# Softmax weighting with V stationary in four column tiles, one group of four heads at a time, turned back by one DMA transposition

## The chip, the cores and the metric

The kernel runs on one core of a Trainium2 chip. The metric is device time in microseconds (us), as the median of the runs of one kernel. The engines are called as in the profile: PE (TensorE matmul) and PEld (its weight loads), DVE (VectorE), ACT (ScalarE), POOL (GpSimd), SP (SyncE, which here only issues DMAs). SBUF is the working memory, PSUM the memory that PE's results go to; a bank is a piece of PSUM that holds one 128x512 fp32 tile here.

## The reference

`x` has 2048 rows of D = 640, in bf16. It is normalised by a layer norm and goes through two branches, whose product is added to `x`:

```python
xn = layernorm(x)
# branch A: 32 heads of Dh = 20, four segments of L = 512 rows
for s in range(4):
    p = softmax(qs @ ks.T * scale + causal_mask)          # inside the segment
    a_dot = p @ vs
    a_mem = (phi(qs) @ M) / (phi(qs) @ z + 1e-6)          # memory of earlier segments
    o = g * a_mem + (1 - g) * a_dot                       # g = sigmoid(beta), one per head
    M += phi(ks).T @ vs;  z += phi(ks).sum(rows)
s = concat(o) @ wo
# branch B: gated linear unit, F = 1536
g = silu((sigmoid(xn @ w_gate) * (xn @ w_up)) @ w_down)
out = x + s * g
```

## The kernel before

**Segments and slots.** The four segments follow each other. Each has 20 slots: four pairs of head groups (a group is four heads, so there are eight groups) times five score batches, `UNITS`. A slot begins with one batch, `scores`: for four heads at once, in four row tiles of the PE array (24 rows each), it writes scores transposed, keys on the partitions, into `Sps`, a PSUM tile of four banks that exists once. ACT takes the exponential of all four banks in one instruction (L527) into `pt` in SBUF, and POOL masks the diagonal blocks of `pt` in place (L530). The causal lower half is never computed, so a group has ten blocks of 128 keys by 128 queries per head: 512 + 384 + 256 + 128 = 1280 query columns. Batches 0 and 3 of `UNITS` hold 512 columns of one group each; batch 1 holds the 128 and 384 of the first group, batch 4 those of the second, and batch 2 the 256 of both.

**Weighting.** `weigh` (L535 on) multiplies by V. For each block and head one matmul has the 128x128 block of `pt` as the stationary operand and the head's 21 columns of `V` (20 and a column of ones) as the moving one, into `Aps`, one PSUM bank that exists once: 40 matmuls a group. The 21st column gives the softmax denominator. After a group's last block DVE takes the reciprocal (L553), multiplies by 1 - g (L554), and writes the product into `od` (L556), with queries on the partitions. A batch is weighed one slot after its scores, in the middle of that slot; the second part of batch 2 one slot later still (`due`, `held`).

**Around it.** The rest of a segment's work is put between by two means. Tasks with a time (in slots) lie in heaps: `at(time, cost, fn)`, and `later` for steps that follow others. Those that cost PE time (`tasks`: V, K and Q projections, the output projection `o_proj`, the memory's read and update) may run in both halves of a slot, those of no cost (`soft`: DMAs, DVE and ACT steps) only in the second half. The gated unit's matmul groups are `bulk`: `gate` and `up` (five matmuls of 512 columns, 1.09 each in the planner) and `down` (twelve of 320, 1.64). A planner gives each slot a level of PE time: `level` minus what the slot already holds, `fixed`, of which `PASS` is the part for weighting. 45% of a slot's share (`FIRST`) is run straight after the scores, then the weighting that is due, then `phi` steps, then soft tasks and the rest:

```python
pt = scores(n, pair, u)
delay[0] = True
goal += FIRST * share
fill(now + 0.45, (tasks,))
flush()
for w in due:
    weigh(*w)
```

All other PSUM tiles come from `ps_d`, three banks in rotation (`dtile`). A `gate` bank is released by ACT's tanh (L431), an `up` bank by DVE (L442), a `down` bank by ACT (L459) and then DVE (L461). While `delay[0]` is true, projections are copied out by DVE, otherwise by ACT (`evacuate`).

**DMAs.** Nearly all are issued by SP, in program order: loads, the store of K and Q to DRAM and their return in another layout (`stage_out` L310, `relay` L274, `c_in` L353), and three families of DMA transpositions: `xn` into `xnT` (L263, L265), `phi(k)` into `pkt` (L378, 128x512 bf16 each), `od` into `oT` (L475, four a segment). `o_ready` adds the memory's part to `od` and lets `o_turn` issue the latter; `o_proj` reads `oT`.

Of the kernel before, what the change touches and what calls it, by code (L numbers as in the profile page):

```python
# [9 lines left out]
P = 128  # L10
S = 2048
D = 640
H = 32
DH = 20
VW = DH + 1
KR = DH + 4
NSEG = 4
L = 512
F = 1536
DC = D // P  # L20
FC = F // P
NG = 8
# [4 lines left out]
BF = mybir.dt.bfloat16  # L27
F32 = mybir.dt.float32
U16 = mybir.dt.uint16
ACT = mybir.ActivationFunctionType  # L30
ALU = mybir.AluOpType
# [19 lines left out]
NU = len(UNITS)  # L51
NSLOT = NG // 2 * NU
WARM = 40
FIRST = 0.45
PASS = [0.41, 0.41, 0.41, 0.2, 0.61]
R = NSLOT / 24


@with_exitstack
def kernel(  # L60
# [14 lines left out]
    nc = tc.nc  # L75
# [3 lines left out]
    cpool = ctx.enter_context(tc.tile_pool(name="const", bufs=1))  # L79
# [3 lines left out]
    lnp = ctx.enter_context(tc.tile_pool(name="ln", bufs=2))  # L83
    xpool = ctx.enter_context(tc.tile_pool(name="xpool", bufs=2))
    stg = ctx.enter_context(tc.tile_pool(name="stg", bufs=1))
    ptp = ctx.enter_context(tc.tile_pool(name="ptp", bufs=3))
    opool = ctx.enter_context(tc.tile_pool(name="opool", bufs=2))
    gpool = ctx.enter_context(tc.tile_pool(name="gpool", bufs=2))
    fpool = ctx.enter_context(tc.tile_pool(name="fpool", bufs=2))
# [13 lines left out]
    def at(time, cost, fn, *a):  # L103
        count[0] += 1
        heapq.heappush(first if fn is phi else tasks if cost > 0.1 else soft, (time, count[0], cost, fn, a))
# [75 lines left out]
                            base=0, pattern=[[-1, P]], channel_multiplier=1)  # L181
    V = []
    for i in range(8):
        va = cpool.tile([P, H, VW], BF, name=f"va{i}")
        V.append(va)
    QT = [cpool.tile([P, 4, L], BF, name=f"QT{i}") for i in range(3)]
    KT = [cpool.tile([P, 4, L], BF, name=f"KT{i}") for i in range(3)]
    nInd = cpool.tile([P, DC, H], F32, name="nInd")
# [3 lines left out]
    def v_ones(a, b):  # L192
        for i in range(a, b):
            nc.gpsimd.memset(V[i][:, :, DH:VW], 1.0)

    def make_ind():

# [116 lines left out]
    def q_chunk(n, c):  # L314
        s = st[n]
        if c == 0:
            s["q5"] = stg.tile([P, DC, L], BF, name="q5")
            s["aq"] = stg.tile([P, DC, L], BF, name="aq")
        ps = dtile([P, L], F32, "psq")
        for k in range(DC):  # L320
            nc.tensor.matmul(ps[:], lhsT=W["q"][:, k, c * P:(c + 1) * P], rhs=s["xnT"][:, k, :],  # L321
                             start=(k == 0), stop=(k == DC - 1))
        (nc.vector.tensor_copy if n else nc.scalar.copy)(s["q5"][:, c, :], ps[:])
        nc.vector.tensor_scalar(s["aq"][:, c, :].bitcast(U16), s["q5"][:, c, :].bitcast(U16), 0x7FFF, None,
                                op0=ALU.bitwise_and)
        if c in (2, 4) and n:
            later(0.9, stage_out, n, c // 4, Qs, QT, "q5")
# [141 lines left out]

    def o_turn(n, j, parts):  # L470
        if "oT" not in st[n]:
            st[n]["oT"] = fpool.tile([P, 4, DC, P], BF, name="oT", bufs=1)
        dst = st[n]["oT"][:, j, 0:parts, :]
        src = st[n]["od"][:, j, 0:parts * P]
        later(0.7, lambda: nc.sync.dma_start_transpose(dst, src))  # L475
# [58 lines left out]
    def weigh(n, pair, u, dg, pt):  # L534
        s = st[n]  # L535
        g = 2 * pair + dg
        first = (u, dg) in ((0, 0), (2, 1))
        if first:
            s["A"] = ps_a.tile([P, 4, 4, VW], F32, name="Aps")
        A = s["A"]  # L540

        mine = [(kb, c0) for (d, kb, c0, ncol) in UNITS[u] if d == dg]
        blocks = [(kb, c0 + (qb - kb) * P, qb) for (kb, c0) in mine for qb in range(kb + 1, 4)]
        blocks += [(kb, c0, kb) for (kb, c0) in mine]
        for (kb, off, qb) in blocks:
            for r in range(4):
                nc.tensor.matmul(A[:, qb, r, :], lhsT=pt[:, r, off:off + P],  # L547
                                 rhs=V[4 * (n % 2) + kb][:, 4 * g + r, :],
                                 start=first, stop=True, skip_group_check=True)
                first = False  # L550
        if (u, dg) in ((2, 0), (4, 1)):
            rd = opool.tile([P, 4, 4], F32, name="rd", bufs=3)
            nc.vector.reciprocal(rd[:], A[:, :, :, DH])  # L553
            nc.vector.tensor_tensor(rd[:], rd[:], gin["omg"][:, 4 * g:4 * g + 4].unsqueeze(1).to_broadcast([P, 4, 4]),  # L554
                                    op=ALU.mult)
            nc.vector.tensor_tensor(  # L556
                s["od"][:, :, 4 * g * DH:(4 * g + 4) * DH].rearrange("p q (r e) -> p q r e", e=DH),
                A[:, :, :, 0:DH], rd[:].unsqueeze(3).to_broadcast([P, 4, 4, DH]), op=ALU.mult)


    bulk = [(1.09, fn, (0, f)) for f in range(FC) for fn in (gate, up)]
# [77 lines left out]
    for n in range(NSEG):  # L639
        w = NSLOT * n  # L640
        m = n + 1
        if m < NSEG:
            if n:
                for p in range(2):
                    for i in range(2):
                        at(w + (-1.4, -0.7, 0.1, 0.55)[2 * p + i], 0.1, ln_stats, m, p, i, i + 1)
                        at(w + (0.6, 0.9, 1.7, 2.0)[2 * p + i], 0.1, ln_norm, m, p, i)
            for i in range(8):
                at(w + R * (3.5 + (0.6 * i if i < 4 else 2.5 + 0.55 * (i - 4))), 0.68, v_tile, m, i // 2, i % 2)
            for c in range(DC):  # L650
                at(w + R * (8.8 + 1.0 * c if n else 9.4 + 0.9 * c), 1.08, k_chunk, m, c)
                at(w + R * (13.8 + 1.1 * c), 1.08, q_chunk, m, c)
                if m + 1 < NSEG:
                    at(w + R * (12.8 + 0.85 * c), 0.0, phi, m, "k5", c)
                at(w + R * (17.4 + 0.8 * c), 0.0, phi, m, "q5", c)
            at(w + R * 19.2, 0.6, q_bound, m)
            if m + 1 < NSEG:
                for p in range(2):
                    at(w + R * (16.1 + p), 0.0, x_load, m + 1, p)
            if n == 0:  # L660
                for c in range(DC):
                    at(R * (2.6 + 0.8 * c), 0.0, phi, 0, "k5", c)
            for i, cs in enumerate(([0, 1, 2], [3, 4])):
                at(w + (9.05, 11.0)[i], 0.75 - 0.25 * i, m_update, n, cs)
        if n >= 1:
            for j in range(4):
                at(w + R * (1.1 + 0.3 * j), 0.0, o_ready, n - 1, j)
                at(w + R * (4.0 + 0.5 * j if j < 3 else 9.6), 0.0, xr_load, n - 1, j)
            for i in range(8):
                at(w + R * (5.4 + 1.1 * i), 0.68, o_proj, n - 1, i // 2, i % 2)  # L670
                at(w + (R * (3.4 + 0.85 * i) if i < 6 else i + 1.55), 0.25, mem_read, n, i // 2, i % 2)
# [13 lines left out]
        while tasks or soft or first:  # L685
            run_task(min((h for h in (tasks, soft, first) if h), key=lambda h: h[0][:2]))

    due, held = [], []
    for n in range(NSEG):
        st[n]["od"] = opool.tile([P, 4, D], BF, name="od")  # L690
        if n:
            bulk += [(1.09, fn, (n, f)) for f in range(FC) for fn in (gate, up)]
        bulk += [(1.64, down, (n, j, h)) for j in range(4) for h in range(2)]
        keep = 4 if n >= NSEG - 2 else 0

        left = sum(b[0] for b in bulk[:len(bulk) - keep])
        fixed = [PASS[i % NU] + sum(t[2] for t in tasks if i <= t[0] - NSLOT * n < i + 1) for i in range(NSLOT)]
        level = min(fixed)
        while sum(max(level - f, 0.0) for f in fixed) < left:
            level += 0.01  # L700
        given, goal = 0.0, 0.0

        def fill(until, heaps):
            nonlocal given
            while True:
                ready = [h for h in heaps if h and h[0][0] < until]
                if ready:
                    run_task(min(ready, key=lambda h: h[0][:2]))
                if len(bulk) > keep and given + 0.5 * bulk[0][0] <= goal:
                    cost, fn, a = bulk.pop(0)  # L710
                    given += cost
                    fn(*a)
                elif not ready:
                    break

        for slot in range(NSLOT):
            pair, u = divmod(slot, NU)
            now = NSLOT * n + slot
            share = max(level - fixed[slot], 0.0)
            pt = scores(n, pair, u)  # L720
            delay[0] = True
            goal += FIRST * share
            fill(now + 0.45, (tasks,))
# [3 lines that stand above are left out]
            delay[0] = False  # L727
            while first and first[0][0] < now + 1.0:
                run_task(first)
            due, held = held, []  # L730
            due.append((n, pair, u, UNITS[u][0][0], pt))
            if u == 2:
                held.append((n, pair, u, 1, pt))
            goal += (1.0 - FIRST) * share
            fill(now + 1.0, (tasks, soft))
        while len(bulk) > keep:
            cost, fn, a = bulk.pop(0)
            fn(*a)
# [47 lines left out]
```

## Time and profile before

| | |
|---|---|
| Time, median of 3 runs (lowest to highest) | 337.55 us (337.18 to 338.45) |
| Profiled execution: span, first to last instruction | 335.5 us |
| PE, ACT, DVE, POOL busy | 328.2, 226.2, 223.1, 111.4 us |
| Weighting: L547, PE | 1280 matmuls, 44.5 us busy, 173 ns each (pipelined) |
| Exponentials: L527, ACT | 80, 150.1 us, 1877 ns each |
| Granted TensorE clock, mean | 0.999 |

For the profiled execution the page gives the span alone. The runs' median lies 2.05 us above that span, and that much is taken to lie around it. A PE matmul's duration in the profile runs from its start to the end of its pipeline, so neighbours overlap; what a matmul costs PE is the distance from its start to the next one's start. ACT and DVE instructions overlap too, by about 0.1 us. The segments' first score batches start at 32.8, 101.0, 181.6 and 255.9 us; the last slot's work ends near 318 us.

### The profile page before, as it was taken

Reading aid. Unit: us, or ns where it says so; the run is one execution under the profiler, and the core shown is the slowest. Engines: PE = TensorE matmul, PEld = TensorE weight load, DVE = VectorE, ACT = ScalarE, POOL = GpSimd, SP = SyncE. Lnnn points to the kernel's source line nnn. Section 1 sums busy time; section 2 is a strip of 40 time slices with the busy share of each in tenths; the row PEclk is TensorE's granted clock in tenths of the full one; section 3 lists DMA queues with packets and bytes.
Section 4 is the critical chain, followed back from the end, with each engine's and each line's share of the span. In section 5 each row is a group of like instructions: output and inputs, shape, how many; then the busy total and the mean of one; then the engine's idle time right before and its main releaser. Section 6 shows DMA issues by size and latency. Waiting matters only on the chain.

```text
span 335.5 us, 8363 instructions
## 1 busy us (share of the span) xinstructions
PE 328.2 (98%) x3402; PEld 187.0 (56%) x3402; DVE 223.1 (66%) x532; ACT 226.2 (67%) x237; POOL 111.4 (33%) x157
## 2 busy tenths in 40 slices
PE   8999899999999999999999999999999999999995
PEld 7544455555664565654566466654556665544673
DVE  6276356589877677788756977875663686643365
ACT  2653797788786676477686676466887776786730
POOL 6636232323226222332233523342222323223214
PEclk9999999999999999999999999999999999999999
DMA  7955993774821631136720452052220621210032
GB/s 236 355 179 174 292 127 67 235 217 113 201 74 21 119 99 41 49 109 92 223 73 2 57 117 85 25 165 76 72 70 3 90 75 37 77 42 3 2 62 78
DMA packets 54725, 35.53 MB, mean 106 GB/s; under 512 B 28576, under 2 KB 54688, under 8 KB 54688
## 3 DMA queue, kind: packets, MB, share of 16 engines
q1 hardware_dynamic: 52480, 32.23, 38.3%
q10 hardware_dynamic: 2208, 2.79, 2.5%
q8 instruction: 26, 0.43, 0.6%
q14 instruction: 11, 0.09, 0.1%
HBM read 20.19 MB, written 8.39 MB: 85 GB/s over the span
## 4 chain that ended last, share of the span: by engine, by line
PE 85%; DVE 6%; DMA 3%; ACT 2%; issue 1%; SPq 1%; POOL 0%; DVEq 0%; ACTq 0%; POOLq 0%
PE up L438 14%; PE gp L428 14%; PE yp L456 12%; PE Aps L547 9%; PE Sps L522 7%; PE sp L502 7%; PE psk L289 7%; PE psv L360 6%; PE psq L321 5%; DMA Wu<-in_B_w_up_dram 2%; PE wps L571 2%; PE dm L388 1%; PE am L410 1%; DMA Qs<-q 1%; DVE q L374 1%
## 5 line engine op out<-in xcount | busy, mean ns | idle before, releaser
L527 ACT ACTIVATE pt<-Sps 128x2048 bf16<-128x2048 f32 x80 | 150.1, 1877 | 28.2 <-PE Sps L522 26.1
L530 POOL TENSOR_SCALAR_AFFINE_SELECT pt<-pt 128x1024 bf16<-128x1024 bf16 (+1 forms) x80 | 76.8, 960 | 196.4 <-ACT pt L527 196.4
L438 PE MATMUL up<-xnT,Wu 128*128 128x512 bf16 x240 | 59.7, 379 | 0.7 <-DMA Wu<-in_B_w_up_dram 0.7
L428 PE MATMUL gp<-xnT,Wg 128*128 128x512 bf16 x240 | 59.6, 379 | 0.2
L442 DVE SCALAR_TENSOR_TENSOR hT<-tg,up 128x512 bf16<-128x512 bf16 x48 | 32.7, 682 | 36.8 <-PE up L438 30.9
L456 PE MATMUL yp<-Wd,hT 128*128 128x320 bf16 x384 | 57.1, 299 | 0.0
L547 PEld LDWEIGHTS <-pt 128*128 128x128 bf16 x1280 | 43.2, 96 | 14.7 <-DVE od L556 1.3
L431 ACT ACTIVATE tg<-gp 128x512 bf16<-128x512 f32 x48 | 28.6, 596 | 27.4 <-PE gp L428 25.1
L547 PE MATMUL Aps<-va,pt 128*128 128x21 bf16 x1280 | 44.5, 173 | 0.4 <-DVE od L556 0.4
L456 PEld LDWEIGHTS <-hT 128*128 128x128 bf16 x384 | 35.4, 97 | 15.2 <-issue 2.4
L438 PEld LDWEIGHTS <-Wu 128*128 128x128 bf16 x240 | 21.2, 97 | 24.2 <-issue 2.6
L461 DVE SCALAR_TENSOR_TENSOR aa<-t,yp 128x320 bf16<-128x320 bf16 x32 | 15.5, 484 | 27.4 <-ACT t L459 27.3
L428 PEld LDWEIGHTS <-Wg 128*128 128x128 bf16 x240 | 21.0, 97 | 21.8 <-issue 1.7
L522 PE MATMUL Sps<-QT,KT 24*128 24x128 bf16 (+3 forms) x512 | 31.7, 301 | 0.3
L459 ACT ACTIVATE t<-yp 128x320 bf16<-128x320 f32 x32 | 14.0, 438 | 19.6 <-PE yp L456 18.4
L360 PE MATMUL psv<-Wv,xnT 128*128 128x320 bf16 x160 | 26.4, 299 | 0.1
L502 PE MATMUL sp<-Wo,oT 128*128 128x320 bf16 x160 | 25.9, 300 | 0.0
L321 PE MATMUL psq<-xnT,Wq 128*128 128x512 bf16 x100 | 24.3, 380 | 0.0
L289 PE MATMUL psk<-xnT,Wk 128*128 128x512 bf16 x100 | 24.2, 379 | 0.0
L522 PEld LDWEIGHTS <-KT 24*128 24x128 bf16 x512 | 9.2, 92 | 23.4 <-issue 21.7
L504 DVE SCALAR_TENSOR_TENSOR aa<-aa,sp 128x320 bf16<-128x320 bf16 x32 | 15.5, 485 | 7.6 <-PE sp L502 7.5
L502 PEld LDWEIGHTS <-oT 128*128 128x128 bf16 x160 | 14.4, 97 | 8.2 <-issue 2.6
(74 smaller groups left out, 327.5 us busy)
## 6 DMA issues: line engine op xcount, KB each, us to landing
KT<-Ks SPq DMA_DIRECT2D x32, 80.0 KB
QT<-Qs SPq DMA_DIRECT2D x32, 80.0 KB
xr<-in_A_x_dram SPq DMA_DIRECT2D x15, 160.0 KB
out_dram<-xr SPq DMA_DIRECT2D x15, 160.0 KB
xt<-in_A_x_dram SPq DMA_DIRECT2D x6, 320.0 KB
Wg<-in_B_w_gate_dram SPq DMA_DIRECT2D x3, 640.0 KB
Wu<-in_B_w_up_dram SPq DMA_DIRECT2D x3, 640.0 KB
Wd<-in_B_w_down_dram ACTq DMA_DIRECT2D x1, 1920.0 KB
```

Source lines behind the costliest of these rows:

```text
L289: nc.tensor.matmul(ps[:], lhsT=W["k"][:, k, c * P:(c + 1) * P], rhs=s["xnT"][:, k, :], start=(k == 0), stop=(k == DC - 1))
L321: nc.tensor.matmul(ps[:], lhsT=W["q"][:, k, c * P:(c + 1) * P], rhs=s["xnT"][:, k, :], start=(k == 0), stop=(k == DC - 1))
L360: nc.tensor.matmul(ps[:], lhsT=s["xnT"][:, k, j * P:(j + 1) * P], rhs=W["v"][:, k, half * HB:(half + 1) * HB], start=(k == 0), stop=(k == ...
L428: nc.tensor.matmul(gp[:], lhsT=Wg[f // 4][:, k, fo:fo + P], rhs=s["xnT"][:, k, :], start=(k == 0), stop=(k == DC - 1))
L438: nc.tensor.matmul(ps[:], lhsT=Wu[f // 4][:, k, fo:fo + P], rhs=s["xnT"][:, k, :], start=(k == 0), stop=(k == DC - 1))
L442: empty(lambda: nc.vector.scalar_tensor_tensor(out=h[:], in0=tg[:], scalar=1.0, in1=ps[:], op0=ALU.add, op1=ALU.mult))
L456: nc.tensor.matmul(yp[:], lhsT=s["hT"][f][:, j * P:(j + 1) * P], rhs=W["d"][:, f, hs], start=(f == 0), stop=(f == FC - 1))
L502: nc.tensor.matmul(sp[:], lhsT=s["oT"][:, j, c, :], rhs=W["o"][:, c, hs], start=(c == 0), stop=(c == DC - 1))
L522: nc.tensor.matmul(Sps[:, r, c0:c0 + ncol], lhsT=kt[32 * r:32 * r + KR, gi, kb * P:(kb + 1) * P], rhs=qt[32 * r:32 * r + KR, gi, kb * P:L] ...
L527: nc.scalar.activation(pt[:], Sps[:], ACT.Exp, scale=SCALE)
L530: nc.gpsimd.affine_select(out=diag, in_=diag, compare_op=ALU.is_ge, fill=0.0, base=0, pattern=[[0, 4], [0, cnt], [1, P]], channel_multipli ...
L547: nc.tensor.matmul(A[:, qb, r, :], lhsT=pt[:, r, off:off + P], rhs=V[4 * (n % 2) + kb][:, 4 * g + r, :], start=first, stop=True, skip_grou ...
```

## The change

For 30 of the 32 groups the weighting is done per group, with the operands exchanged. `weigh_group` holds V stationary: for each of the four key blocks, four matmuls, one per head, each with 32 columns of V (the head's 21 and the first 11 of the next head, for which V gets one more head of ones) in one of four column tiles of the PE array, and up to 512 columns of `pt` moving. The 16 matmuls of a group write one PSUM bank, `AT`, with the four heads on the partitions and the queries along the row. ACT copies it to `ats` in bf16, one DMA transposition (SP) turns it into `A` in SBUF, with queries on the partitions, and `divide` does the three DVE instructions that `weigh` did, now from `A`.

The place in the order changes as well. A group is weighed straight behind a score batch: the first group of a pair behind batch 3, the second behind batch 0 of the next pair. The transposition is a soft task 0.7 slots after the slot's start, the division one 1.45 slots after. The last pair of the last segment keeps the old way. The planner's `PASS` gives way to `TURN = 0.65` in the slots that weigh. `pt` has four buffers instead of three; `od` has one buffer instead of two, and `oT` shares its place with `aq`. `o_ready` moves from 0.92 to 1.67 slots into the next segment to 1.7 to 2.45.

```diff
+TURN = 0.65
+LAST = (NSEG - 1, NG // 2 - 1)
...
-    ptp = ctx.enter_context(tc.tile_pool(name="ptp", bufs=3))
+    ptp = ctx.enter_context(tc.tile_pool(name="ptp", bufs=4))
...
-        va = cpool.tile([P, H, VW], BF, name=f"va{i}")
-        V.append(va)
+        V.append(cpool.tile([P, H + 1, VW], BF, name=f"va{i}"))
...
             nc.gpsimd.memset(V[i][:, :, DH:VW], 1.0)
+            nc.gpsimd.memset(V[i][:, H, 0:DH], 1.0)
...
-            s["aq"] = stg.tile([P, DC, L], BF, name="aq")
+            s["aq"] = stg.tile([P, DC, L], BF, name="aq", tag="aq")
...
-            st[n]["oT"] = fpool.tile([P, 4, DC, P], BF, name="oT", bufs=1)
+            st[n]["oT"] = stg.tile([P, 4, DC, P], BF, name="oT", tag="aq")
...
         if (u, dg) in ((2, 0), (4, 1)):
-            rd = opool.tile([P, 4, 4], F32, name="rd", bufs=3)
...
+            divide(n, g, A)
+
+    def divide(n, g, A):
+        s = st[n]
+        if "od" not in s:
+            s["od"] = opool.tile([P, 4, D], BF, name="od", bufs=1)
+        rd = opool.tile([P, 4, 4], F32, name="rd", bufs=3)
+        nc.vector.reciprocal(rd[:], A[:, :, :, DH])
+        nc.vector.tensor_tensor(rd[:], rd[:], gin["omg"][:, 4 * g:4 * g + 4].unsqueeze(1).to_broadcast([P, 4, 4]),
+                                op=ALU.mult)
+        nc.vector.tensor_tensor(
+            s["od"][:, :, 4 * g * DH:(4 * g + 4) * DH].rearrange("p q (r e) -> p q r e", e=DH),
+            A[:, :, :, 0:DH], rd[:].unsqueeze(3).to_broadcast([P, 4, 4, DH]), op=ALU.mult)
+
+
+    def weigh_group(now, n, pair, dg, pts):
+        g = 2 * pair + dg
+        AT = ps_a.tile([P, L], F32, name="AT", tag="A")
+        mine = sorted((kb, u, c0, ncol) for u in range(NU) for (d, kb, c0, ncol) in UNITS[u] if d == dg)
+        for i, (kb, u, c0, ncol) in enumerate(mine):
+            v = V[4 * (n % 2) + kb][:].rearrange("p h e -> p (h e)")
+            for r in range(4):
+                h0 = (4 * g + r) * VW
+                nc.tensor.matmul(AT[32 * r:32 * r + 32, kb * P:L], lhsT=v[:, h0:h0 + 32],
+                                 rhs=pts[u][:, r, c0:c0 + ncol],
+                                 start=(i == 0), stop=(i == 3), tile_position=(0, 32 * r))
+        ats = opool.tile([P, L], BF, name="ats", bufs=2)
+        nc.scalar.copy(ats[:], AT[:])
+        A = opool.tile([P, 4, 4, 32], BF, name="Asb", bufs=2)
+        at(now + 0.7, 0.0, lambda: nc.sync.dma_start_transpose(A[:].rearrange("p q r e -> p q (r e)"), ats[:]))
+        at(now + 1.45, 0.0, divide, n, g, A)
...
-                at(w + R * (1.1 + 0.3 * j), 0.0, o_ready, n - 1, j)
+                at(w + 1.7 + 0.25 * j, 0.0, o_ready, n - 1, j)
...
+    def passes(n, i):
+        pair, u = divmod(i, NU)
+        turned = TURN if u == 3 and not old(n, pair) or u == 0 and (n or pair) else 0.0
+        return turned + (PASS[u] if old(n, pair) and u else 0.0)
...
             pt = scores(n, pair, u)
+            if u == 0 and (n or pair):
+                q = n * (NG // 2) + pair - 1
+                weigh_group(now, q // (NG // 2), q % (NG // 2), 1, pts)
+                pts = {}
+            pts[u] = pt
+            if u == 3 and not old(n, pair):
+                weigh_group(now, n, pair, 0, pts)
...
-            due.append((n, pair, u, UNITS[u][0][0], pt))
-            if u == 2:
-                held.append((n, pair, u, 1, pt))
+            if old(n, pair):
+                due.append((n, pair, u, UNITS[u][0][0], pt))
+                if u == 2:
+                    held.append((n, pair, u, 1, pt))
```

## The prediction

> **What bounds the kernel now.** First the page's totals and its chain of waits; after the span, shares of the span by engine:
>
> ```profile
> span 335.5 us, 8363 instructions
> ...
> PE 328.2 (98%) x3402; PEld 187.0 (56%) x3402; DVE 223.1 (66%) x532; ACT 226.2 (67%) x237; POOL 111.4 (33%) x157
> ...
> PE 85%; DVE 6%; DMA 3%; ACT 2%; issue 1%; SPq 1%; POOL 0%; DVEq 0%; ACTq 0%; POOLq 0%
> ```
>
> PE is the bound, so PE time saved counts unless a wait takes its place. An average hides where, so next the windows by segment (columns: window; length, then busy us of PE, PEld, DVE, ACT, POOL; clock; DMA share; GB/s), and two dense stretches:
>
> ```profile
> 32.80:101.00 68.20, 66.71 (x738) 37.31 (x737) 46.87 (x100) 55.59 (x59) 19.27 (x20) 1.00 0.70 167
> 101.00:181.60 80.60, 80.60 (x848) 45.52 (x847) 59.46 (x144) 55.01 (x57) 25.86 (x36) 1.00 0.36 86
> 181.60:255.90 74.30, 74.20 (x800) 41.16 (x799) 54.14 (x131) 51.03 (x48) 24.14 (x32) 1.00 0.30 76
> 255.90:318.00 62.10, 62.02 (x725) 35.19 (x725) 34.53 (x85) 46.21 (x40) 17.55 (x19) 1.00 0.19 44
> ...
> 72.00:98.00 26.00, 25.77 (x289) 15.21 (x285) 22.94 (x48) 21.20 (x26) 8.46 (x8) 1.00 0.58 145
> 132.00:162.00 30.00, 30.00 (x299) 15.47 (x296) 25.56 (x58) 19.60 (x20) 8.86 (x12) 1.00 0.40 95
> ```
>
> In the first segment ACT is at 82%; in the two stretches DVE is at 88 and 85%, and in the first of them the chain in order of time lies on DVE (79.6 to 84.6, 88.7 to 91.4 us). There PE time saved is worth little. Third, PE's timeline of one window (start, us, instruction):
>
> ```profile
> 241.01 0.33 PE L522 MATMUL Sps<-QT,KT 24*128 24x384 bf16 x4
> 241.27 0.60 PE L334 MATMUL cps<-aq,IK 128*32 128x512 bf16 x5
> 241.81 1.25 PE L428 MATMUL gp<-xnT,Wg 128*128 128x512 bf16 x5
> 242.90 0.56 PE L547 MATMUL Aps<-va,pt 128*128 128x21 bf16 x16
> 243.31 0.38 PE L438 MATMUL up<-xnT,Wu 128*128 128x512 bf16 x1
> ```
>
> This has the price of the old weighting (16 in 243.31 - 242.90), of a 512-column matmul (five in 242.90 - 241.81), and a column-tiled product: `cps`, four tiles and then the first again, 32 columns each. Last, a slot's rhythm:
>
> ```profile
> 39.76 0.40 PE L522 MATMUL Sps<-QT,KT 24*128 24x256 bf16 x8
> 40.36 1.87 ACT L527 ACTIVATE pt<-Sps 128x2048 bf16<-128x2048 f32 x1
> 42.30 1.10 POOL L530 TENSOR_SCALAR_AFFINE_SELECT pt<-pt 128x1024 bf16<-128x1024 bf16 x1 [2.69 <-ACT pt L527]
> ```
>
> The next batch can overwrite `Sps` 2.44 us after a batch began (the shortest slots of the trace are 2.44), and `pt` is masked 3.64 us after (43.40 - 39.76).
>
> **Part by part.** *Removed:* 40 matmuls a group at 0.41/16 = 25.6 ns, 1.025 us; 30 groups, 30.8 us.
>
> *Added on PE:* 1280 columns a group if the four heads run side by side. 1.09/5/512 = 0.426 ns a column makes 0.545 us. `cps` took 0.54 for two rounds of 512 (0.436), so 0.10 is the change of tiling. 0.645 us a group, 30 groups 19.4. One after another the tiles would take 2.18 + 0.10; `cps` says not, since its five would have taken 1.09. PE net: **-11.4**.
>
> The Trainium skill ("TensorE: Matmul & The Clock Gate", Measured speedup vs the span model) gives three column tiles of 512 columns a speedup of 2.38, not 3. By that share, as an estimate, four would give 3.17 and a group 0.79 us, so that PE would win 7.1 and not 11.4. The trace disagrees: the five of `cps` in 0.54 are a full four.
>
> *Moved: waits for the mask.* The old weighting of a batch came in the middle of the next slot; now it stands straight behind that slot's scores, where PE has nothing else to do. For the first group of a pair, batch 2 is the late one and is needed after scores (0.33) and two rounds (0.38): PE waits when slot 2 is shorter than 3.64 - 0.71 = 2.93. For the second it is batch 4, after 0.33 and one round: below 3.09. The slots' lengths follow from the kernel's own planner: fixed tasks, weighting and the bulk groups that fall to the slot, plus 0.40 for the scores. For the kernel before that gives 3.67, 3.05, 3.87 for slots 2 to 4 of the first segment, and the trace has 3.68, 3.07, 3.88. For the changed one, short before a weighting are: slot 9 of the first segment (2.23), 14 of the third (2.57), 2, 4, 9 and 14 of the last (2.29, 2.67, 2.17, 2.58). Lifted to 2.44 where shorter, they wait 0.65, 0.52, 0.49, 0.42, 0.65, 0.51: 3.2. Slots under 2.44 wait for `Sps` itself: five, together 1.0, against 0.5 before (2.09 and 2.24). **+3.7**; bounds 1.5 (half the short slots fill up from delays elsewhere) and 5.
>
> *Added on ACT:* 30 copies of 128x512 fp32; the same form, `cb` L337, took 0.58: 17.4 us. In the queue a copy stands behind that slot's exponential, so PE's matmuls are done before ACT gets there; behind it stand the tanh that release `gate` and `down` banks. By segment ACT would hold 59.7 of 64.9, 59.6 of 77.6, 55.6 of 71.3 and 50.3 of 59.8 us. Slack covers it except in the first segment. There slots 2 to 5 hold four exponentials, two copies, five `phi` exponentials (0.63), two tanh (0.6) and four casts (0.43), 14.7 us less 0.1 overlap each, 13.0, in 12.0 us of PE work, and slots 15 to 17 hold 9.5 in 8.5. Part of that can run late: **+1.7**; bounds 0.5 and 4 (half the deficit of an ACT-bound segment).
>
> *Added on SP, DMA and DVE:* the nearest row is the transposition of `pkt`, the same shape: 15 of them held SP 1.19 us at the median, and by the semaphore steps of the trace landed 2.3 to 2.6 us after issue on quiet queues, 3.5 to 4.3 on busy ones. `ats` is ready 3.05 us after the slot's start (2.47, then 0.58), so `A` lands at 5.5 to 7.3. The division is queued on DVE for the second half of the next slot, which DVE reaches at 4.5 to 6. So DVE, in order, waits up to 2 us, and behind it are queued the `hT` and `aa` evacuations that free `ps_d`'s banks, and `phi`'s DVE steps. PE feels that only after two more tiles (2 x 1.09 + 0.33 less 0.68 for L442): some 1.8 us are free, and a DVE that is behind doesn't wait at all. Not covered are three kinds of groups. The first, where SP is held:
>
> ```profile
> 46.36 1.34 SPq L353 DMA_DIRECT2D QT<-Cs  x4
> 47.80 8.76 SPq L378 DMA_TRANSPOSE pkt<-k  x5
> ```
>
> its transposition, due at 46.9, gets behind one of `pkt`, issues at 49 and lands at 52, while DVE is free at 48: 1.2 us on PE. The first group of the second and third segments, which gets behind eight transpositions of `xnT` and `oT` (106.96 to 117.4 before, now 0.8 slots later): 0.4 each. Two groups in the stretch 72 to 98, where DVE is the chain: 0.35 each. **+2.7**; bounds 0 and 12 (a third of the groups at 1.2). What waits on SP behind a transposition (`relay`, `stage_out`, `pkt`) was planned a slot ahead of its use, `o_proj` comes 2 slots after the last `oT`; if that cover were gone, each would cost its 1.2.
>
> *At nothing:* the divisions have the same shapes (0.25 + 0.24 + 0.49), from SBUF; extra memsets lie beside the startup; shared `aq` and `oT` are free half a slot before reuse; `od`'s one buffer is free before the first division, which waits longer for `A`. Bounds -1 and +1.
>
> Sum: -11.4 + 3.7 + 1.7 + 2.7 = -3.3 on the profiled execution, 332.2 for a span of 335.5. With the 2.05 that lie around it: **334.2 us**.
>
> **Rivals.** *All waits are hidden (14%).* Delays lengthen the short slots, so masks are ready, and DVE's waits stay inside the 1.8 us. -11.4 plus 1.5 and 1.5: 329.2. For it: PE shows hardly a stall in the middle segments. Against: the short slots come out of the planner's costs.
>
> *The savings are eaten just so (16%).* ACT in the first segment and DVE in its second half hold the time, so that segment's 3.6 is lost and its waits remain: 337.5.
>
> *The division's wait becomes the bound: slower (27%).* A transposition that lands 4 us after issue, as pkt's did at 153.9, behind one other on SP (1.2), puts `A` at 8.3 us while DVE is there at 5: 3.3 against the 1.8 that the banks allow. It decides once DVE's wait passes 1.8 us. If ten groups pay 1.5 each and the DVE stretches (56 us, at 87%) lose another 2, the sum is -11.4 + 3.7 + 1.7 + 17 = +11, at half of that +2.5: 340 to 348.5, of which 343 is taken. Against: the DMA share is 0.36 and less after the first segment.
>
> *The four tiles don't run side by side (5%).* With 128 rows from four places of `pt` at a share of 3/4, a group costs 0.83 and PE wins 5.9: 339.7; one after another, 2.28 a group, 375 (1%). `cps` speaks against both.
>
> **How the numbers follow.** The forecast has 38%, the rivals 14, 16, 27 and 5. Faster are forecast and first rival, 0.52; the second, 0.16, is no change within 0.5% (1.7 us, about what runs of this kernel can tell: they lie 1.3 apart); slower 0.32. The range 329 to 343 leaves out the lower half of the first rival (7%) and the upper part of the slow ones (12%). The forecast's own range is 331 to 336.
>
> **What would show it.** Right: 480 column-tiled matmuls whose groups lie 0.64 us from first to next work; PE waiting for POOL's mask of batches 2 and 4 in the last segment, some 3 us in all; 30 copies of 0.58 on ACT; DVE waiting for transpositions 15 to 30 us, with little of it on the chain. Wrong: groups over 0.8 us on PE; DVE's wait for `A` on the chain with more than 2%; a first segment longer than 68.2; a PE without waits for POOL.

## The result and the profile after: 3.8% slower

The changed kernel took 351.2 us (median of 5 runs, 349.12 to 355.49), the kernel before 337.55: 1.038 times as long, interval 1.0339 to 1.042. The forecast was 334.2, its range 329 to 343. The result lies outside, on the other side. The ratio leaves out the slowest of the five runs, 355.49, and as that run was the profiled one, the profile shown here is that of a second run of the same file (`x0_after` below, 350.52 us in its profiled execution).

The page, cut to totals, PE's clock in 40 slices and the chain of waits by engine:

```profile
span 348.5 us, 6990 instructions
...
PE 321.4 (92%) x2649; PEld 166.5 (48%) x2682; DVE 227.0 (65%) x532; ACT 239.8 (69%) x267; POOL 111.2 (32%) x165
...
PEclk9999999999999999999999998999999989999998
...
PE 68%; DVE 9%; DMA 7%; ACT 7%; issue 4%; SPq 2%; POOL 2%; ACTq 0%; DVEq 0%
```

PE is busy 6.8 us less and idle 27.1 us instead of 7.3 (span less busy). PE's part of the chain fell from 85 to 68%, that of DMA rose from 3 to 7%; by line, the transpositions `Asb<-ats` alone hold 4.0% of the chain. Two slices inside the span show a lower clock.

The windows by segment (columns as before; last, the last segment with the start of what follows it):

```profile
33.20:105.60 72.40, 63.97 (x535) 31.84 (x541) 48.09 (x97) 58.18 (x66) 19.72 (x21) 1.00 0.73 169
105.60:186.80 81.20, 77.92 (x643) 40.05 (x651) 61.13 (x144) 58.88 (x65) 24.60 (x34) 1.00 0.43 99
186.80:264.50 77.70, 73.40 (x596) 36.22 (x603) 54.12 (x134) 54.66 (x56) 24.47 (x33) 0.98 0.36 85
264.50:330.70 66.20, 62.39 (x574) 31.83 (x581) 35.44 (x86) 49.64 (x47) 17.65 (x19) 0.97 0.23 55
```

Measured from first score batch to first score batch (in the last segment, to the start of its last slot), the segments take 72.4, 81.2, 77.7 and 64.2 us, against 68.2, 80.6, 74.3 and 60.2. In the first two PE is busy 2.7 us less than before, in the third 0.8, part of it at a lower clock, and each segment is longer all the same. So each has waits that are new. From the table of waits (engine, line, what it waited for: us in total, times, longest):

```profile
PE sp L504 <- DVE aa L506: 4.6, 2, 2.3
PE Sps L524 <- ACT pt L529: 3.4, 5, 2.0
PE AT L577 <- POOL pt L532: 2.1, 6, 0.4
...
DVE rd L561 <- DMA Asb<-ats: 20.6, 11, 3.8
```

POOL's masks (`AT L577 <- POOL pt`) were forecast. The few long waits at `sp` were not. One of them, in the third segment, in the timeline (start, us, engine, instruction, in brackets the idle time before it and what ended it):

```profile
202.02 2.55 SPq L477 DMA_TRANSPOSE oT<-od  x2
204.62 0.57 SPq L495 DMA_DIRECT2D xr<-in_A_x_dram  x1
205.29 1.20 SPq L583 DMA_TRANSPOSE Asb<-ats  x1
206.26 0.85 PE L362 MATMUL psv<-Wv,xnT 128*128 128x320 bf16 x5
207.99 0.25 DVE L561 RECIPROCAL rd<-Asb 128x16 f32<-128x16 bf16 x1 [3.79 <-DMA Asb<-ats]
208.90 0.48 DVE L506 SCALAR_TENSOR_TENSOR aa<-aa,sp 128x320 bf16<-128x320 bf16 x1
209.43 1.26 PE L504 MATMUL sp<-Wo,oT 128*128 128x320 bf16 x5 [2.31 <-DVE aa L506]
```

It reads from the top. SP issues two transpositions of `oT` and a load before it comes to the first group's own. That one lands 2.7 us after its issue (205.29 to 207.99). DVE has stood still before the reciprocal for 3.79 us by then. The next instruction in DVE's order that PE needs is `aa` L506, which frees a `ps_d` bank, and PE, with its other banks full, starts again 0.53 us after that began.

### The profile page after: what moved, and what is told of

Read it like the earlier page. It is cut to its first block, busy times and chain, and to the rows that moved or that the text cites. A ratio compares the mean times of both kernels' runs of the same rounds, so it can differ in the third digit from the quotient of the medians.

```text
span 353.4 us, 6990 instructions
## 1 busy us (share of the span) xinstructions
PE 325.6 (92%) x2649; PEld 168.1 (48%) x2682; DVE 226.7 (64%) x532; ACT 239.9 (68%) x267; POOL 111.1 (31%) x165
## 4 chain that ended last, share of the span: by engine, by line
PE 61%; DVE 13%; DMA 10%; ACT 7%; issue 5%; SPq 2%; POOL 2%; ACTq 0%; DVEq 0%
PE yp L458 12%; PE up L440 10%; PE gp L430 9%; PE psk L291 6%; PE sp L504 5%; DMA Asb<-ats 5%; PE Sps L524 5%; ACT pt L529 4%; PE AT L577 4%; PE psv L362 3%; PE psq L323 3%; DMA Wu<-in_B_w_up_dram 2%; DVE k L376 2%; PE dm L390 1%; DMA Qs<-q 1%
## 5 line engine op out<-in xcount | busy, mean ns | idle before, releaser
L440 PE MATMUL up<-xnT,Wu 128*128 128x512 bf16 x230 | 60.9, 388 | 6.2 <-DVE aa L506 2.4
L458 PE MATMUL yp<-Wd,hT 128*128 128x320 bf16 x384 | 55.9, 299 | 0.1
L440 PEld LDWEIGHTS <-Wu 128*128 128x128 bf16 x240 | 22.8, 99 | 32.6 <-issue 8.6
L524 PE MATMUL Sps<-QT,KT 24*128 24x128 bf16 (+3 forms) x512 | 32.7, 308 | 3.6 <-ACT pt L529 3.5
L430 PEld LDWEIGHTS <-Wg 128*128 128x128 bf16 x240 | 22.2, 98 | 27.8 <-issue 4.7
L504 PE MATMUL sp<-Wo,oT 128*128 128x320 bf16 x160 | 26.7, 306 | 4.8 <-DVE aa L506 4.8
L362 PE MATMUL psv<-Wv,xnT 128*128 128x320 bf16 x160 | 27.1, 306 | 0.7 <-ACT tg L433 0.5
L577 PE MATMUL AT<-pt,va 128*32 128x512 bf16 (+1 forms) x480 | 24.0, 313 | 1.7 <-POOL pt L532 1.6
L561 DVE RECIPROCAL rd<-Asb 128x16 f32<-128x16 bf16 x30 | 7.4, 247 | 23.1 <-DMA Asb<-ats 22.9
L303 DVE TENSOR_REDUCE kabs<-k 128x1 f32<-128x512 bf16 x20 | 13.6, 680 | 9.3 <-ACT k L282 9.3
```

Source lines behind the costliest of these rows:

```text
L362: nc.tensor.matmul(ps[:], lhsT=s["xnT"][:, k, j * P:(j + 1) * P], rhs=W["v"][:, k, half * HB:(half + 1) * HB], start=(k == 0), stop=(k == ...
L430: nc.tensor.matmul(gp[:], lhsT=Wg[f // 4][:, k, fo:fo + P], rhs=s["xnT"][:, k, :], start=(k == 0), stop=(k == DC - 1))
L440: nc.tensor.matmul(ps[:], lhsT=Wu[f // 4][:, k, fo:fo + P], rhs=s["xnT"][:, k, :], start=(k == 0), stop=(k == DC - 1))
L458: nc.tensor.matmul(yp[:], lhsT=s["hT"][f][:, j * P:(j + 1) * P], rhs=W["d"][:, f, hs], start=(f == 0), stop=(f == FC - 1))
L504: nc.tensor.matmul(sp[:], lhsT=s["oT"][:, j, c, :], rhs=W["o"][:, c, hs], start=(c == 0), stop=(c == DC - 1))
L524: nc.tensor.matmul(Sps[:, r, c0:c0 + ncol], lhsT=kt[32 * r:32 * r + KR, gi, kb * P:(kb + 1) * P], rhs=qt[32 * r:32 * r + KR, gi, kb * P:L] ...
```

## The experiments

The theories carry letters in the expectations. A: DVE, in order, waits for the transposition, and what stands behind the division holds PE. B: 30 more transpositions crowd SP and the DMA engines. C: ACT's copies, or the new weighting on PE, cost more than was thought. P: of what remains, the place of the division in DVE's order is the cause. M: it is the waits for the masks. Q: the transpositions hold up other transfers on SP's queue, so that ACT and DVE run late in the first segment. A' and B' ask the same as A and B of a division that is queued later.

**Taking the steps out, one behind the other.** `x0_after` is the changed kernel again. `x1_const_div` divides from a constant tile, so the transposition is issued and nobody waits for it. `x2_no_turn` doesn't issue it either, `x3_no_copy` also leaves out ACT's copies. In the last three the output lacks the weighting's result.

```diff
+    A0 = cpool.tile([P, 4, 4, 32], BF, name="A0")
+    nc.gpsimd.memset(A0[:], 1.0)
...
-        ats = opool.tile([P, L], BF, name="ats", bufs=2)          # x3
-        nc.scalar.copy(ats[:], AT[:])                             # x3
-        A = opool.tile([P, 4, 4, 32], BF, name="Asb", bufs=2)     # x2, x3
-        at(now + 0.7, 0.0, lambda: nc.sync.dma_start_transpose(...))   # x2, x3
-        at(now + 1.45, 0.0, divide, n, g, A)
+        at(now + 1.45, 0.0, divide, n, g, A0)
```

> The changed kernel as it is, as the level for the others and for a second trace. Theory A (DVE, in order, waits for the transposed group; PE runs out of banks for 2 to 3 us and its clock is then granted at half for 3.4 us): 351 us, again with four or five PE gaps over 2 us, and a granted clock under 0.99. Theory B (the transpositions crowd SP's queue and the DMA engines, so that other transfers come late) and theory C (the weighting itself, its waits for POOL and the copies on ACT cost what was saved) expect the same time.

> The division reads a constant tile instead of the transposed one, so that DVE never waits for the transposition; everything else, the transposition too, is issued as before (the softmax part of the output is left out by this). Theory A: the gaps at the first group of the second, third and last segment (2.4, 2.6, 2.5 us) and one in the first go, with their half-clock stretches (1.7 us each): 351 falls to about 338. Theory B and theory C: nothing of theirs is touched, 348 or more.

> As the one with the constant tile, and the transposition isn't issued at all (the softmax part is left out). Theory A: within 2 us of the run with the constant tile. Theory B: a further clear fall, since the gap of 3.0 us at 64.5 us, where a late pkt transposition holds ACT, goes with its half-clock stretch of 6.8 us: 6 us less, about 332. Theory C: 345 or more, as nothing of PE or ACT is taken away.

> As the one without transposition, and ACT's 30 copies are left out too: the weighting on PE alone remains of the change, with a division that reads a constant. By the prediction's sum this is 337.55 - 11.4 for PE and + 3.7 for the waits for masks: 330. Theory C's ACT part: at least 3 us below the run without transposition; theories A and B: within 1.5 us of it. If PE's part itself were mis-sized, this would stay at 335 or more.

| | us | ratio to before | interval |
|---|---|---|---|
| x0_after | 348.98 | 1.0348 | 1.0279 to 1.0418 |
| x1_const_div | 337.46 | 1.0008 | 0.9988 to 1.0028 |
| x2_no_turn | 337.34 | 1.0014 | 0.9991 to 1.0038 |
| x3_no_copy | 336.81 | 0.9992 | 0.9961 to 1.0023 |

Waiting for the transposition costs 11.5 us (348.98 - 337.46; the runs of `x0_after` spread over 5.0, from 345.82 to 350.82), and without it the loss is gone within the interval. To issue it while nobody waits costs nothing that can be measured (x1 against x2), and the copies 0.5 us, with intervals that overlap. `x3_no_copy`, which the sum had put at 330, took 336.81. A stands; B falls, as far as nobody waits; of C the copies fall. The windows of `x1_const_div`:

```profile
32.70:101.50 68.80, 63.60 (x539) 31.70 (x545) 45.87 (x97) 58.34 (x66) 20.07 (x21) 1.00 0.79 180
101.50:180.20 78.70, 77.75 (x643) 40.01 (x651) 60.14 (x144) 59.15 (x65) 24.93 (x34) 1.00 0.43 101
180.20:253.70 73.50, 71.53 (x600) 35.45 (x607) 54.69 (x134) 54.65 (x56) 24.91 (x33) 1.00 0.38 90
253.70:316.10 62.40, 60.61 (x574) 31.32 (x581) 35.88 (x86) 49.55 (x47) 17.67 (x19) 1.00 0.26 58
```

The wait's price falls on all four segments: 3.6, 2.5, 4.2 and 3.8 us (72.4 - 68.8, and so on). But even without it the kernel only draws level with the one before. PE does over 11 us less work (the table below) and the time isn't shorter. That is a second question, and the other runs go after both.

**Waiting less.** `d1_late` queues each division one slot later, except for a segment's eighth group, whose result `o_ready` needs; `d2_mid` moves the weighting to the middle of the slot, so that it waits for no mask; `d3_late_mid` does both; `d4_one_wait` is `d1_late` with one division of the third segment back in its early place.

```diff
-        at(now + 1.45, 0.0, divide, n, g, A)
+        at(now + (1.45 if g == NG - 1 else 2.45), 0.0, divide, n, g, A)            # d1, d3
+        at(now + (1.45 if g == NG - 1 or (n, g) == (2, 0) else 2.45), 0.0, ...)    # d4
...
-                weigh_group(now, n, pair, 0, pts)
+                todo = (now, n, pair, 0, pts)          # d2, d3; the other call likewise
...
             flush()
+            if todo:
+                weigh_group(*todo)
```

> The division is queued one slot later (2.45 slots after the group's slot instead of 1.45), but for the eighth group of a segment, whose result is needed for o_ready; all else as changed. DVE should find the group already there. Theory A' (the position of the division in DVE's order, ahead of the landing, is what costs 11.5 us): as with the constant tile, 337.5 within 2 us, no PE gap over 2.2 us but the one at about 75 to 80 us. Theory B' (it is the transposition itself, its landing however late, that holds od and what follows): 345 or more.

> The group is weighed in the middle of its slot, where the old weighting stood, instead of straight behind the score batch. Theory M (PE's waits for POOL's mask, 3.1 us in the constant-tile run, come from that place): they go, but the copy comes no earlier, so DVE's waits stay: about 346. Rival: the moved group is ready later, the transposition too, and DVE waits longer by what is saved: 349 or more.

> Both: late division, weighting in the middle of the slot. Theories A' and M together: 337.5 - 3.1 = 334.4, a version below the kernel before. If the masks' 3.1 us are only exchanged for DVE's in-order work (the rival of the constant-tile run, where PE ran into DVE at five places): 337.

> As the late division, but the first group of the third segment keeps its early one. One wait of DVE by itself: theory A' with the half clock: a PE gap of about 2.4 us and 3.4 us at half clock behind it, so 4 us above the late division (341.5). Without a price of the clock: 2.4 us above (340).

Measured: `d1_late` 341.44 us (ratio 1.0133, 1.0103 to 1.0162), `d2_mid` 353.92 (1.0483, 1.0436 to 1.053), `d3_late_mid` 341.89 (1.0134, 1.0072 to 1.0195), `d4_one_wait` 347.61 (1.031, 1.0281 to 1.034). A later division takes back 7.5 of the 11.5 us. What `d1_late` keeps lies in the first segment, 72.6 us against 68.8 in `x1_const_div`; the other three come within 0.8 of it. Weighting in mid-slot brings nothing beside it (d3 as d1), and alone makes it worse: copy and transposition come later then, while the division keeps its place. The clearest is `d4_one_wait`: **one** division in the early place costs 6.2 us (347.61 - 341.44), where 4 was expected. Its waits, and its windows around that place:

```profile
PE sp L504 <- DVE aa L506: 4.1, 1, 4.1
...
DVE rd L561 <- DMA Asb<-ats: 5.9, 2, 5.6
```

```profile
200.00:206.20 6.20, 3.96 (x40) 2.12 (x39) 0.90 (x3) 4.17 (x4) 1.78 (x2) 1.00 0.62 128
206.30:213.20 6.90, 5.18 (x28) 2.62 (x28) 4.45 (x13) 0.90 (x3) 0.00 (x0) 0.51 0.32 90
```

DVE waits 5.6 us, PE 4.1 behind it (until 208.0), and from 206.3 on, before PE's wait is over, its granted clock is 0.51 for 6.9 us. The stall is paid twice, once as idle time and once in the clock. `x0_after` shows the same at the stall above, before, at and after it:

```profile
206.00:209.30 3.30, 1.12 (x18) 0.61 (x10) 1.24 (x5) 2.14 (x2) 0.68 (x1) 1.00 0.66 181
209.70:213.10 3.40, 3.40 (x17) 2.06 (x15) 2.57 (x8) 0.43 (x1) 0.00 (x0) 0.50 0.22 65
213.20:216.60 3.40, 3.25 (x27) 1.80 (x27) 0.88 (x3) 2.28 (x2) 0.75 (x1) 1.00 0.19 48
```

In the stretch of the middle row one 128x320 matmul of `psv` takes PE 0.267 us from start to start, in that of the last row 0.136. It has a second such stretch at 284.8, behind another wait for `aa` (2.0 us, until 284.1).

**A complete version without the wait.** `e1_mid_div` queues the division in the middle of the slot two slots later, where the transposition should long have landed, with `o_ready` moved to fit. `e2_mid_both` adds weighting in mid-slot, `e3_q_later` also moves the second part of `phi(q)` by half a slot, since in `d1_late` DVE waited 2.39 us there for a store. `e4_middle_segs` is `e3_q_later` with the old weighting in the first and last segments. `f3_turn_wide` is `e1_mid_div` with a planner that allots 1.3 to a weighting slot, so that fewer are short.

```diff
-        at(now + 1.45, 0.0, divide, n, g, A)
+        divs.append((now + 2, n, g, A))
...
-                at(w + 1.7 + 0.25 * j, 0.0, o_ready, n - 1, j)
+                at(w + 2.5 + 0.05 * j, 0.0, o_ready, n - 1, j)
...
             flush()
+            while divs and divs[0][0] <= now:
+                divide(*divs.pop(0)[1:])
...
-        later(0.8, rest)
+        later(0.8 if src == 'k5' else 1.3, rest)      # e3, e4
...
-        return (n, pair) == LAST
+        return n in (0, NSEG - 1)                     # e4
...
-TURN = 0.65
+TURN = 1.3                                            # f3
```

> As changed, but the division is queued in the middle of the slot two slots later, behind the evacuations that PE waits for (o_ready moves to 2.5 slots). Theory P (what is left after DVE's wait for the transposition is the division's place in DVE's order: a PE gap of 2.1 us near 75 us, and the ACT and DVE lateness of the late-division run): 336, at or below the kernel before. Rival Q (the transpositions hold up the Qs and pkt transfers on SP's queue, so that ACT and DVE run late in the first segment, whatever the place): 340 or more, with a first segment of 71 us or more against 68.2.

> As the one with the division in the middle, and the group weighed in the middle of its slot too. Theory M, on top of P: the waits for POOL's mask (3.7 us) go, 332 to 333. If the late-division pair repeats itself (masks exchanged for other waits): within 1 us of the run with the division in the middle.

> As the last, and phi's DVE steps on q come half a slot later, behind the landing of the Qs store. Rival Q's part: DVE's wait for Qs in the first segment (2.4 us in the late-division run), which held ACT and then PE at about 95 us for 1.9 us with 3.4 us of half clock, goes: 3 us below the run before. Theory P alone: the same within 1 us.

> As the last, but the first and the last segment keep the old weighting; only the second and third, 16 groups, are weighed with V stationary. If the saving on PE counts only where ACT and DVE leave room, these two segments give about 16 x 0.37 = 6 us and the others lose nothing: 332. If the whole kernel can use the saving: 3 to 4 us slower than the run before.

> A complete kernel: the division in the middle of the slot two slots later, and TURN at 1.3 instead of 0.65, so that the planner puts fewer bulk groups into the slots that weigh and more into those ahead of them. The mask's waits (3.5 us in the run with the division in the middle) go: 336.5. If PE only meets other waits in their place: 339 or more.

Measured: 340.17 us (ratio 1.0094, 1.0069 to 1.0119), 340.04 (1.0106, 1.0058 to 1.0153), 340.12 (1.0112, 1.0073 to 1.0151), 345.08 (1.0251, 1.022 to 1.0281), 340.65 (1.0117, 1.0088 to 1.0145). DVE's wait for the transposition falls from 20.6 us to 1.8 in e1, 2.3 in e2, and 0.3 in e3 and f3, and 1% of loss stays. Neither the weighting in mid-slot (e2, where no wait for a mask is left) nor longer slots (f3, where these waits fall from 2.4 to 1.3 us) changes that, so M falls. P's 336 for e1 was missed; Q's 340 was met, its first segment of 71 us or more nearly (70.4). `e3_q_later` gains nothing, but it doesn't settle Q: DVE still waits 0.9 us for the store in its trace, as in that of e2, and PE 1.8 us for `Sps` at 95.5. `e4_middle_segs` was a miss: its middle segments took 80.4 and 75.9 us, about the 80.6 and 74.3 of the kernel before, and its last one 65.8, with a wait for the single `od` buffer (3.3 us on DVE, 3.9 on PE).

**What is PE's saving worth?** `f1_pe_only` leaves out copies, transpositions and divisions of the 30 groups, so that only the exchanged matmuls remain; `f2_pe_only_mid` puts these in mid-slot; `f4_x1_mid_div` is `x1_const_div` with the division placed as in `e1_mid_div`. All three outputs lack the weighting's result.

```diff
-        ats = opool.tile([P, L], BF, name="ats", bufs=2)      # f1, f2: down to the division
...
-        at(now + 1.45, 0.0, divide, n, g, A)
+        if g == 1:
+            st[n]["od"] = opool.tile([P, 4, D], BF, name="od", bufs=1)
+            nc.gpsimd.memset(st[n]["od"][:], 1.0)
```

> PE's 480 matmuls alone: no copy, no transposition and no division for the 30 groups (od is set to a constant once a segment; the softmax part is left out). Theory P (PE's saving was lost to DVE's in-order work around the division, 4.9 us, and to masks and Sps, 4.8 us): 5 us under the kernel before, 332. If the DVE waits come from other DVE work that PE runs into, and not from the divisions: 336.

> As the last, with the group weighed in the middle of the slot, so that masks are ready. Theories P and M together: nearly all of PE's 11 us, 328. If PE then only runs into the next wait: 331 or more.

> The constant tile, with the division in the middle of the slot two slots later (o_ready at 2.5 slots). Theory P: the 2.1 us gap near 75 us and the smaller ones go, 334. If the division's work, not its place, is what PE runs into: 337.

Measured: `f1_pe_only` 333.54 us (ratio 0.9909, 0.9875 to 0.9942), `f2_pe_only_mid` 332.61 (0.9872, 0.9855 to 0.9889), `f4_x1_mid_div` 338.29 (1.0046, 1.0031 to 1.0061). f4 says that P falls too: with nothing to wait for, the later division is no better than the early one. And f1 gives the answer that surprised most. With every cost of the new evacuation left out, PE's saving brings 3 to 4 us. Its segments take 66.7, 78.5, 73.0 and 60.4 us, against 68.2, 80.6, 74.3 and 60.2: the last one gains nothing.

To see where the rest went, PE's time is summed from each matmul's start to the next one's, by tile, from 33 us on, in the profiled executions; so a wait counts with the tile ahead of it:

| us on PE | before | f1_pe_only | f2_pe_only_mid | x1_const_div | x0_after |
|---|---|---|---|---|---|
| weighting, `Aps` and `AT` | 33.65 | 24.92 | 22.42 | 25.63 | 25.59 |
| scores, `Sps` | 27.21 | 26.24 | 26.38 | 26.12 | 26.83 |
| `am`, `dm`, `cps` (the memory) | 11.11 | 13.26 | 13.19 | 14.17 | 14.27 |
| `gp`, `up`, `yp` | 151.58 | 153.16 | 156.19 | 154.33 | 156.12 |
| `psk`, `psq`, `psv` | 52.32 | 54.33 | 53.81 | 53.32 | 61.99 |
| `sp`, `po` | 22.12 | 22.27 | 22.91 | 22.54 | 25.68 |
| all | 297.98 | 294.18 | 294.92 | 296.12 | 310.50 |

(Where a record is missing, its time is its neighbour's. In f1's `psv`, 1.2 us are a wait that ends at 36.07, for the transfer of `Wg`.) The new weighting without waits is 30 x 0.659 = 19.8 us and the last pair's old way 2.1, 21.9. f1 has 3.0 above that, the masks. Mid-slot (f2) nearly all of these are gone, 22.4, but `gp`, `up` and `yp` take 3.0 more. Part of what f1 loses elsewhere is seen here, behind the memory's read:

```profile
126.72 0.33 PE L412 MATMUL am<-Mbd,q 128*128 128x84 bf16 x3
126.92 0.49 DVE L280 CAST va<-psv 128x320 bf16<-128x320 f32 x1 [1.27 <-PE psv L362]
127.47 1.02 PE L430 MATMUL gp<-xnT,Wg 128*128 128x512 bf16 x4 [0.42 <-DVE va L280]
```

`am` keeps PE for only some 0.2 us, and `gp` needs a `ps_d` bank that DVE is still copying out. In the trace of before, that place had `am` and then 0.49 us of old weighting (127.65 and 127.82, then the scores at 128.31), which writes a bank of its own. So the old matmuls were also PE work that needs no `ps_d` bank while the engines emptied those banks. That this is the reason was read at this place; it was not tested.

## Why the prediction was wrong

**PE net -11.4: right as work.** Scores and a group take 0.986 us from the first start to the next work, scores alone 0.327: a group is 0.659, forecast 0.645. In `x0_after`:

```profile
105.62 0.40 PE L524 MATMUL Sps<-QT,KT 24*128 24x512 bf16 x4
105.94 0.73 PE L577 MATMUL AT<-pt,va 128*32 128x512 bf16 x16
106.61 1.25 PE L430 MATMUL gp<-xnT,Wg 128*128 128x512 bf16 x4
```

0.67 here (106.61 - 105.94). 31.5 us were removed (33.65 - 2.12) and 19.8 added: -11.7. The four tiles run side by side, and that rival is out. The Trainium skill's 2.38 for three tiles ("TensorE: Matmul & The Clock Gate", Measured speedup vs the span model), which by the estimate made 0.79 of a group, does not hold here: the trace has 0.659.

**Masks and `Sps` +3.7: right.** The six mask waits came at the slots named, 0.60, 0.53, 0.44, 0.22, 0.60 and 0.45 in f1 (between starts, in the order of the forecast's 0.65, 0.52, 0.49, 0.42, 0.65, 0.51); `x0_after` has a seventh of 0.4, in the first segment. But taking them away (f2) gained 0.9 us, within the intervals: a wait taken out here mostly came back elsewhere.

**ACT +1.7: too high.** 30 copies of 0.58 as forecast, 0.5 us by x2 against x3.

**Two smaller numbers.** The 2.05 us taken to lie around the span are 1.7 in a run of the kernel before (336.71 with a span of 335.0) and 2.1 in the changed one (351.2 with 349.1). And 375 for tiles one after another leaves out the 8.1 us of waits that the number beside it, 339.7, holds.

**The step that failed: "Added on SP, DMA and DVE", +2.7.** It measured 11.5. What it said of the parts was right: `A` lands 2.7 to 4.3 us after issue (205.29 to 207.99; 49.69 to 54.00), the transposition holds SP 1.20, DVE waits 20.6 us (forecast 15 to 30), and the first group of a segment gets behind the transpositions of `oT`. Its upper bound, 12, just held. The bound of 1.8 us of free waiting was of the right kind: seven of DVE's eleven waits are 1.9 us or less and cost little. The other four are those of the first group of each segment, 2.27, 3.28, 3.79 and 2.97 us, and the sizes put on these were wrong in three ways. The second and third take 2.3 us each from PE; they were put at 0.4. That of the last segment, behind its own `oT`, takes 2.0 and was left out; that of the first takes 2.9 and was put at 1.2. And the half clock behind such a gap was not priced at all. The 9.5 us of idle PE at these four places and two stretches of 3.41 us at half clock, worth 1.7 each, are 12.9 of the 14.6 us between the spans of these executions of x0 and x1 (348.5 - 333.9).

In the first segment the price sits at 64 us, where `Sps` waits 2.0 and then 0.9 us for ACT. The chain leads from there to a transposition of `pkt` (58.58), from that to the `phi` steps on DVE, and from these to the division that waited for `A` until 54.02. `x1_const_div` issues the same transpositions in the same order and has no such gap, so this price too comes with DVE's wait. The profile names nothing for the last 3.7 us before ACT goes on at 64.05.

**A second step failed, hidden by the first.** Without its +2.7 the sum was -6.0; x1, which has all but the wait, gave +0.3 by its ratio. Of PE's 11.7 only 3 to 4 us appear even where the evacuation is left out (f1, f2). The sum took all of it but the waits that it listed; that the old matmuls also covered the emptying of banks is the reading above, not a tested cause. The rival "the savings are eaten just so" named this size, 337.5, for ACT in the first segment and DVE in its second half. That its number was met is luck as to the place: against the kernel before, x1 has lost part or all of PE's saving in each segment (68.8, 78.7, 73.5 and 60.5 us, against 68.2, 80.6, 74.3 and 60.2). Of what doesn't appear, 2.8 us go with the divisions (x3 against f1 by their ratios), although the kernel before had the same three instructions per group.

**Which case came true.** The division's wait became the bound (27%), at four places instead of ten groups, and each dearer: 351.2 where 343 was taken and 348.5 was its end. Of the signs of "wrong", two appeared: `A` on the chain with more than 2% (4.0), and a first segment longer than 68.2 (72.4).

**Open:** the 2.7 us by which e1 to e3 stay above x1 (by the ratios of e1 and x1 2.9, of which f4, with the later place alone, has 1.3), and what exactly eats the rest of PE's saving in f1. All runs but that of the kernel before also have a later `o_ready`, the shared buffers and a planner that allots `TURN`; none of these was taken back by itself, so they stay rivals of the reading with the banks.

## What to carry to other kernels

A result that now returns through a DMA may be read by an in-order engine only when it has surely landed: look at the worst place, where the issuing queue is full, since one such wait cost 6.2 us here while most cost little. Matmuls that write a bank of their own may be cover for the emptying of the others; of the PE work saved there, about a third showed here, so its worth is measured rather than counted. Such a run (here f1) is cheap, and sets the most that any mending of the rest can bring.

## What the runs showed of the chip that was not expected

Gaps of 2.0 and 2.3 us on PE were enough for the granted clock to fall to 0.5, for 3.41 us (at 209.71 and 284.80 in `x0_after`). In `d4_one_wait` a gap of 4.1 us came with 6.83 us of it. Three gaps of the same length (2.0 until 66.55, 2.0 until 81.47 and 2.3 until 129.37 in `x0_after`) were followed by none. The traces show what sets them apart. Their granted clock changes only at whole steps of 3.413 us from its first change, and each trace can be cut into these steps. Three of `x0_after`:

```profile
62.93:66.34 3.41, 1.60 (x8) 0.61 (x7) 0.69 (x1) 2.21 (x2) 0.00 (x0) 1.00 1.06 359
127.78:131.20 3.42, 1.77 (x14) 1.13 (x14) 3.25 (x10) 0.36 (x2) 0.58 (x1) 1.00 0.44 117
206.30:209.71 3.41, 1.10 (x12) 0.67 (x9) 1.62 (x6) 1.84 (x2) 0.68 (x1) 1.00 0.68 180
```

PE is idle for 1.81, 1.65 and 2.31 us of them (length less busy), and only the last is followed by half clock. The edge of a step cuts the gaps at 66.55, 81.47 and 129.37 in two; the other two lie within one step each. In the 18 traces of this case, from 33 us on, all twelve steps at full clock with 2.06 us or more of idle PE were followed by half clock, one of the three with 1.83 to 1.99 was, and none with less. So it was the idle time within one step that counted, and where the steps lie differs from one execution to the next: the gap of 2.0 us before `up`, spared at 81.47 here, was struck at 83.99 in the first profile of the same kernel.

The Trainium skill ("TensorE: Matmul & The Clock Gate", Part 1) tells of a free-running window of about 3.4 us, and that a window of idleness halves the clock. The steps of 3.413 us agree with the window's length; as to the idleness the measurement decides, and here some 2 us of one window were enough.
